# Spreading out the key work of later batches and reordering the head of a fused attention and MLP kernel

## The chip, the cores and the metric

The kernel runs on one core of one Trainium2 chip. The metric is the device time of one execution in microseconds (us), smaller is better. A time is the median of four to six timed executions (of one for m_csplit); a profile is what the hardware profiler recorded of one execution, and its span, from the first to the last instruction, is some 2 us shorter than the time. TensorE (PE in the profile) is the matrix engine, VectorE is DVE, ScalarE is ACT, GpSimd is POOL, and SP is the engine that issues most DMA transfers.

One thing has to be known about TensorE to follow this document. It has two clocks, and in every trace here the fast one was granted only some time after TensorE had begun to work. The trace holds a record of each grant. In the kernel before, pairs of 64-column passes start 107 ns apart up to 10.5 us and 57 ns apart from 10.6 us. I call the moment of the grant "the release" and the time before it "cold".

## The reference

Attention with a polynomial sketch, without softmax, then a two-layer MLP with the ELU activation. Four batches, four heads, 1088 rows, head dimension 32, sketch size r = 8.

```python
def phi(x):                                   # x: (b, h, s, 32)
    a = np.einsum('rd,bhsd->bhsr', S1, x)
    b = np.einsum('rd,bhsd->bhsr', S2, x)
    return np.einsum('bhsi,bhsj->bhsij', a, b).reshape(*x.shape[:-1], 64)
q_p, k_p = phi(q), phi(k)
kv  = np.einsum('bhsf,bhsd->bhfd', k_p, v)
z   = np.sum(k_p, axis=2)
num = np.einsum('bhsf,bhfd->bhsd', q_p, kv)
den = np.einsum('bhsf,bhf->bhs', q_p, z)[..., None] + 1e-06
x   = (num / den).transpose(0, 2, 1, 3).reshape(4352, 128)
h   = x @ w_in                                # 128 -> 2048
g   = np.where(h > 0, h, np.exp(np.minimum(h, 0)) - 1)
out = g @ w_out                               # 2048 -> 128
```

Nearly all the arithmetic is in the MLP. The attention decides when the MLP can start, and it must then be slipped in between the MLP's matmuls without making them wait.

## The kernel before

The kernel issues every instruction in a fixed order by hand. It has a head, which brings the first batch to its first MLP group, and a body of steps, each of two MLP matmul groups, one of each layer (1.72 us each), plus small pieces of attention work that are hung on numbered steps.

The head:

```python
def keep_warm(n, cols=256):                    # fillers: their results are never read
    for i in range(n):
        nc.tensor.matmul(idle[:, :cols], some[:, :P], some[:, :cols], skip_group_check=True)
...
eps = const.tile([1, 8, D + 1], F32, name="eps")      # one row: 1e-6 in the denominator's column
...
load_hd(nc.sync, "k", k, 0, 0, KT)             # keys of batch 0: two loads, runs of 1152 and 1024 B
load_hd(nc.scalar, "k", k, 0, KT, NT)
load_hd(nc.sync, "q", q, 0, 0, 8, slice(0, 1))
load_hd(nc.scalar, "q", q, 0, 0, 8, slice(1, 2))
load_v(0)
...
keep_warm(3)
keep_warm(1, 160)
sps = psum.tile([P, 512], F32, name="sps", tag="aux")
nc.tensor.matmul(sps[:, :2 * R], Sx[:]..., ident[:2 * R, :2 * R])
make_SX()                                      # one more matmul, 8 rows
...
def x0_eps():                                  # starts the sums of the first queries with 1e-6
    xps = []
    for tt in range(2):
        p = psum.tile([P, 512], F32, name="x0ps", tag="h", bufs=4)
        nc.tensor.matmul(p[:, :8 * (D + 1)], some[:1, :P], eps[:].rearrange("p m d -> p (m d)"),
                         start=True, stop=False, skip_group_check=True)
        xps.append(p)
    return xps
...
x0 = x0_eps()                                  # also serves as a filler
transp(kT, "k", 0, 0, KT)                      # VectorE: keys, two halves
transp(kT, "k", 0, KT, NT)
KF(0)                                          # TensorE: key features (abp in the profile)
KF_out(0)                                      # ScalarE: copies of them
transp(qT, "q", 0, 0, 8)                       # VectorE: first queries
KO(0, 0)                                       # VectorE: outer products (kp), group by group
q1_first()                                     # TensorE: query features (abqp)
KO(0, 1)
KO(0, 2)
RA(0)
RB(0)
q2_first()                                     # VectorE: outer product of the queries (qp)
for i in range(3):
    KA(0, i)                                   # TensorE: sums of keys times values (kv)
KC(0)
KZ1(0)
KS0()
q4_first()                                     # TensorE: transposes (qtp)
q5_first(x0)                                   # TensorE: x0ps, then x
mm1_first()                                    # first MLP matmul
```

The body. RA and RB are the first two steps of splitting a weight that arrives as 64-bit numbers; RC is the rest, and its flag sends its last step to GpSimd:

```python
for n, i in ((2, 3), (3, 4), (4, 6), (5, 5), (6, 7), (8, 8), (10, 9), (12, 10)):
    ...
    at(n, RC, i, i > 6)

for b, (n_t, n_f, n_o, n_a, n_z, n_q) in enumerate(
        ((3, 5, (6, 7), 8, 10, 9), (11, 12, (13, 14), 19, 20, 21), (17, 18, (20, 21), 22, 24, 25)), 1):
    at(n_t, transp, kT, "k", b, 0, NT)          # VectorE
    at(n_f, KF_late, b)                         # TensorE, 16 passes of 288 columns
    late(n_f, KF_late_out, b)                   # two VectorE transposes
    for half in range(2):
        at(n_o[half], KO_late, b, half)         # VectorE outer products
    at(n_a, KA_late, b)
    ...
```

## Time and profile before

| | kernel before |
|---|---|
| timed runs | 283.95 us (282.7 to 284.42) |
| span of the profile | 282.1 us |
| release of the TensorE clock | 10.59 us |
| first MLP matmul | 17.81 us |
| first 512-column MLP group | 19.62 us |

The prediction below shows the waits, the chain and the stretches of this profile. One more view is TensorE's own timeline. Its columns are start, duration, engine, source line, operation, output<-inputs, rows*columns of the weights, shape, and number of instructions; in brackets is the idle time ahead of it and who ended it.

```profile
5.59 1.96 PE L554 MATMUL x0ps<-eps,some 1*128 1x264 f32 x4
7.48 2.08 PE L298 MATMUL abp<-Sab,kT 128*64 128x64 f32 x33
...
10.34 2.66 PE L397 MATMUL kv<-v,kp 128*64 128x64 f32 x72
...
14.53 2.00 PE L569 MATMUL x0ps<-kvz,qpT 128*128 128x66 f32 x16
```

TensorE is never idle for long in this head. The 72 kv matmuls begin at 10.34, a quarter of a microsecond before the release, and so take 2.66 us.

### The profile page before, as it was taken

The numbers are of one execution on the slowest core, as the hardware profiler recorded it, in microseconds if no ns is written. First come the engines' busy times: TensorE is split into PE (matmuls) and PEld (weight loads), VectorE is DVE, ScalarE is ACT, GpSimd is POOL, SyncE is SP. The second block draws the span as 40 slices with busy tenths as digits, with TensorE's granted clock in tenths as the row PEclk, the third lists the DMA queues.
The fourth block names the chain that finished last, engine by engine and source line by source line (L and its number), as shares of the span: only waits on it lengthen the run. The fifth ranks groups of instructions, "written<-read, shape, count | busy, mean of one in ns | idle before, by whom it ended". The sixth has DMA issues, their size and how long they took to land.

```text
span 282.1 us, 3800 instructions
## 1 busy us (share of the span) xinstructions
PE 273.7 (97%) x1348; PEld 138.4 (49%) x1348; DVE 178.7 (63%) x319; ACT 179.8 (64%) x337; POOL 20.9 (7%) x55
## 2 busy tenths in 40 slices
PE   8999998999979999999999999999999999999994
PEld 6874333543443545444444444444444444444694
DVE  6788999998947695366635663456445734573442
ACT  2368966676546564666756665666566666667682
POOL 4070004333000000000000000000000000000000
PEclk9999999999999999999999999999999999999999
DMA  6994790010002200002000100020002000110020
GB/s 180 342 330 138 206 261 14 15 67 0 0 2 34 43 1 2 0 4 35 3 0 9 29 2 0 0 33 5 0 2 37 0 1 0 23 17 0 5 33 19
DMA packets 25474, 13.35 MB, mean 47 GB/s; under 512 B 18416, under 2 KB 23664, under 8 KB 25456
## 3 DMA queue, kind: packets, MB, share of 16 engines
q1 hardware_dynamic: 24944, 12.66, 17.5%
q10 hardware_dynamic: 512, 0.46, 0.5%
q8 instruction: 10, 0.16, 0.3%
q14 instruction: 8, 0.07, 0.1%
HBM read 10.88 MB, written 2.23 MB: 46 GB/s over the span
## 4 chain that ended last, share of the span: by engine, by line
PE 87%; DVE 8%; issue 1%; ACT 1%; POOL 1%; POOLq 0%; DVEq 0%
PE h L661 37%; PE o L698 36%; PE ol L721 3%; PE qps L627 2%; DVE gg L685 2%; PE kvl L340 1%; PE idle L221 1%; DVE kp L282 1%; PE qps L492 1%; POOL raw L122 1%; PE x0ps L569 1%; DVE raw L117 1%; PE h L668 1%; PE x0ps L554 1%; DVE W L112 1%
## 5 line engine op out<-in xcount | busy, mean ns | idle before, releaser
L685 DVE SCALAR_TENSOR_TENSOR gg<-e,h 128x512 f32<-128x512 f32 (+1 forms) x144 | 93.2, 656 | 89.5 <-ACT e L679 89.3
L661 PE MATMUL h<-xg,W 128*128 128x512 f32 (+1 forms) x284 | 127.0, 569 | 1.5 <-POOL W L123 1.1
L677 ACT ACTIVATE e<-h 128x512 f32<-128x512 f32 (+1 forms) x144 | 81.1, 564 | 72.6 <-PE h L661 72.4
L698 PE MATMUL o<-gg,W 128*128 128x512 f32 x256 | 121.7, 598 | 0.0
L679 ACT ACTIVATE e<-e 128x512 f32<-128x512 f32 (+1 forms) x144 | 87.3, 606 | 4.6
L661 PEld LDWEIGHTS h<-xg,W 128*128 128x128 f32 x284 | 53.4, 190 | 63.7 <-issue 51.8
L698 PEld LDWEIGHTS o<-gg,W 128*128 128x128 f32 x256 | 47.4, 190 | 56.3 <-issue 55.2
L104 ACT ACTIVATE W<-W,ebias 128x256 uint32<-128x256 uint32 (+1 forms) x11 | 6.6, 600 | 5.7 <-DVE W L99 5.6
L520 DVE TENSOR_TENSOR qp<-an,abw 128x1024 f32<-128x1024 f32 (+1 forms) x9 | 9.3, 1047 | 0.3
L627 PE MATMUL qps<-qpT,kvp 64*64 64x256 f32 (+3 forms) x136 | 7.4, 339 | 1.5 <-DVE qpT L617 1.5
L721 PEld LDWEIGHTS ol<-W,gg 128*128 128x128 f32 x64 | 8.1, 192 | 0.3
L617 DVE STREAM_TRANSPOSE qpT<-qp 128x1024 f32<-128x1024 f32 (+1 forms) x7 | 8.1, 1161 | 0.0
L721 PE MATMUL ol<-W,gg 128*128 128x128 f32 x64 | 8.1, 275 | 0.0
L282 DVE TENSOR_TENSOR kpl<-abk 128x1280 f32<-128x1280 f32 (+1 forms) x6 | 8.1, 1346 | 0.0
L627 PEld LDWEIGHTS qps<-qpT,kvp 64*64 64x64 f32 x136 | 4.7, 132 | 6.6 <-issue 3.1
L122 POOL TENSOR_TENSOR raw<-raw,tiny 128x512 f32<-128x512 f32 x4 | 5.4, 1338 | 32.3 <-DVE raw L117 32.3
L502 DVE STREAM_TRANSPOSE abw<-qps 128x256 f32<-128x256 f32 (+1 forms) x14 | 5.2, 407 | 2.0 <-ACT xg L639 2.0
L117 DVE SCALAR_TENSOR_TENSOR raw<-raw 128x256 f32<-128x256 uint32 (+1 forms) x11 | 6.0, 549 | 0.3
L112 DVE SCALAR_TENSOR_TENSOR W<-raw,W 128x256 uint32<-128x256 uint32 (+1 forms) x11 | 5.9, 541 | 0.0
L705 DVE STREAM_TRANSPOSE ob<-o 128x512 f32<-128x512 f32 x8 | 5.7, 710 | 0.1
L639 ACT COPY xg<-qps 128x256 f32<-128x256 f32 x12 | 3.9, 373 | 2.8 <-PE qps L492 2.8
L123 POOL TENSOR_TENSOR W<-raw,W 128x512 f32<-128x512 f32 x4 | 5.4, 1342 | 0.3
(118 smaller groups left out, 136.2 us busy)
## 6 DMA issues: line engine op xcount, KB each, us to landing
raw<-in_moe_w_in_dram SPq DMA_DIRECT2D x8, 256.0 KB, 5.8
raw<-in_moe_w_out_dram SPq DMA_DIRECT2D x8, 256.0 KB, 5.9
hd_k<-in_k_dram SPq DMA_DIRECT2D x3, 544.0 KB, 8.3
hd_q<-in_q_dram SPq DMA_DIRECT2D x3, 544.0 KB, 3.2
out_dram<-ob SPq DMA_DIRECT2D x40, 32.0 KB, 1.7
v<-in_v_dram SPq DMA_DIRECT2D x4, 288.0 KB, 9.0
v<-in_v_dram SPq DMA_DIRECT2D x4, 256.0 KB, 9.1
hd_k<-in_k_dram SPq DMA_DIRECT2D x1, 288.0 KB, 3.7
```

The lines of the kernel that those rows point to most:

```text
L112: nc.vector.scalar_tensor_tensor(d, hi, 0x80000000, d, op0=AND, op1=OR)
L117: nc.vector.scalar_tensor_tensor(lo.bitcast(F32), lo, 2.0 ** -32, raw[:, :, 1], op0=MUL, op1=ADD)
L122: nc.gpsimd.tensor_mul(mant, mant, _ap(tiny[:], [[0, dst.shape[1]]]))
L282: nc.vector.tensor_mul(dst, _ap(a_, list(a_.ap[1:]) + [[0, R]]), _ap(b_, [b_.ap[1], [0, R], b_.ap[2]]))
L520: nc.vector.tensor_mul(qp[g][:, h], _ap(a_, list(a_.ap[1:]) + [[0, R]]), _ap(b_, [b_.ap[1], [0, R], b_.ap[2]]))
L627: nc.tensor.matmul(ps[e][64 * g2:64 * g2 + 64, 64 * k:64 * (k + m)], kvp[r, b, f, g2].rearrange("p c d -> p (c d)"), qpT[g][r, n * g2 + 2 ...
L661: nc.tensor.matmul(hs[g, cp][c][:, :n], W[:, cp, c * P:c * P + P], xg[g][:, :n])
L677: nc.scalar.activation(e, hs[g, cp][c][:, :n], RELU, scale=-1.0)
L679: nc.scalar.activation(e, e, EXP, scale=-1.0)
L685: nc.vector.scalar_tensor_tensor(gs[g, cp][:, c, :n], es[g, cp][:, c, :n], -1.0, hs[g, cp][c][:, :n], op0=ADD, op1=MAX)
L698: nc.tensor.matmul(ops[g][:, :n], W[:, cp, (2 + c) * P:(3 + c) * P], gg[:, c, :n], start=(first and c == 0), stop=(last and c == 1))
L721: nc.tensor.matmul(ops[g][i][:], gg[:, c, i * P:i * P + P], W[:, cp, (2 + c) * P:(3 + c) * P], start=(first and c == 0), stop=(last and c ...
```

## The change

It has two intents. In the body, VectorE is full up to 80 us and has room afterwards, so the key work of batches 2 and 3 goes to later steps, batch 1 gets its features in a way that needs no VectorE transpose, some small GpSimd work moves, and the last rounding step goes from GpSimd to VectorE for most weights. In the head, the first group of keys is loaded, transposed and turned into features ahead of the rest, so that VectorE's chain of outer products can start 1.5 us earlier; the place of x0ps in front is given to a short filler, and x0ps follows the query features.

```diff
-    load_hd(nc.sync, "k", k, 0, 0, KT)
-    load_hd(nc.scalar, "k", k, 0, KT, NT)
+    load_k0(nc.sync, 0, 0, 4)                  # four loads, by tiles: runs of 512 and 640 B
+    load_k0(nc.scalar, 1, 0, 4)
+    load_k0(nc.sync, 0, 4, KT)
+    load_k0(nc.scalar, 1, 4, NT - KT)
...
-    keep_warm(1, 160)
+    keep_warm(1, 64)
...
     def KF(b):
-        ps = [psum.tile([P, 512], F32, name="abp", tag="aux") for _ in range(2)]
+        ps = [psum.tile([P, 512], F32, name="abp", tag="h", bufs=4) for _ in range(2)]
...
+    def KF_second(b):                          # batch 1: 36 passes of 64 columns, keys as weights
+        ...
+            nc.scalar.copy(ab[:, :, t]..., ps[j][:, :64 * n]...)
...
-    x0 = x0_eps()
-    transp(kT, "k", 0, 0, KT)
-    transp(kT, "k", 0, KT, NT)
+    keep_warm(1, 96)
+    transp(kT, "k", 0, 0, 8)
+    transp(kT, "k", 0, 8, NT)
     KF(0)
     KF_out(0)
+    KO(0, 0)
     transp(qT, "q", 0, 0, 8)
-    KO(0, 0)
     q1_first()
+    x0 = x0_eps()
     KO(0, 1)
+    q2_first()
     KO(0, 2)
     RA(0)
     RB(0)
-    q2_first()
-    for i in range(3):
-        KA(0, i)
+    KA(0, 0)
+    KA(0, 1)
+    q4_first(0)
+    KA(0, 2)
...
-        at(n, RC, i, i > 6)
+        at(n, RC, i, i == 7)
...
-            ((3, 5, (6, 7), 8, 10, 9), (11, 12, (13, 14), 19, 20, 21), (17, 18, (20, 21), 22, 24, 25)), 1):
+            ((3, 5, (7, 9), 10, 11), (15, 16, (17, 18), 19, 20), (18, 20, (24, 25), 27, 29)), 1):
...
-        at(n_f, KF_late, b)
-        late(n_f, KF_late_out, b)
+        if b == 1:
+            at(n_f, KF_second, b)
+        else:
+            at(n_f, KF_late, b)
+            late(n_f, KF_late_out, b)
```

Cut are the index function for the new key positions, the moves of make_SWp, KZ3, KS, make_SXh and of the query transposes, and a change of one accumulation bank.

More of the change, by code (lines that the diff above doesn't have):

```diff
@@ L79, in load_hd, with key_at, load_k0 @@
                       src[b].rearrange("h (a c t) d -> (h a) c t d", a=32, c=2)[:, c, t0:t1, :])
+    def key_at(u, i):
+        return 4 * u + i if i < 4 else 4 * (1 + u) + u + i
+    def load_k0(eng, u, i0, i1):
+        if ("k", 0) not in hd:
+            hd["k", 0] = work.tile([P, 2, NT, D], F32, name="hd_k", tag="hd_k")
+        p = key_at(u, i0)
+        eng.dma_start(hd["k", 0][:, :, p:p + i1 - i0, :],
+                      k[0].rearrange("h (a c t) d -> (h a) c t d", a=32, c=2)[:, :, u * KT + i0:u * KT + i1, :])
     def load_v(b, engs=(nc.sync, nc.sync)):
@@ L297, in KF @@
             for u in range(2 if i + KT < NT else 1):
-                nc.tensor.matmul(to[64 * u:64 * u + 64, :], kT[b][:, u * KT + i, :],
+                nc.tensor.matmul(to[64 * u:64 * u + 64, :], kT[b][:, key_at(u, i), :],
                                  Sab[:].rearrange("p h y -> p (h y)"),
@@ L301, in KF @@
         abps[b] = [where[i] for i in (0, 4, 8)]
+    def KF_second(b):
+        ps = [psum.tile([P, 512], F32, name="abp", tag="aux") for _ in range(2)]
+        for i in range(KT):
+            for u in range(2):
+                nc.tensor.matmul(ps[i // 5][64 * u:64 * u + 64, 64 * (i % 5):64 * (i % 5) + 64],
+                                 kT[b][:, u * KT + i, :], Sab[:].rearrange("p h y -> p (h y)"),
+                                 skip_group_check=True, tile_position=(0, 64 * u))
+        ab = feats[b] = work.tile([P, 2, KT, H, R], F32, name="abk", tag="abk", bufs=2)
+        for j in range(2):
+            t = slice(0, 5) if j == 0 else slice(5, KT)
+            n = t.stop - t.start
+            nc.scalar.copy(ab[:, :, t].rearrange("p x t h r -> p x (t h) r"),
+                           ps[j][:, :64 * n].rearrange("p (m x r) -> p x m r", x=2, r=R))
     def KF_late(b):
@@ L333, in KA_late @@
     def KA_late(b):
-        kv = kv_ps[b] = psum.tile([P, 512], F32, name="kvl", **(dict(tag="aux") if b == 1 else dict(tag="o1", bufs=1)))
+        kv = kv_ps[b] = psum.tile([P, 512], F32, name="kvl", **(dict(tag="aux") if b == 1 else dict(tag=f"o{3 - b}", bufs=1)))
         ab = feats.pop(b)
@@ L539, in q2_first, with q4_first @@
         outer(qp[0][:], abw[0][:])
-    def q4_first():
-        qpT[0] = work.tile([P, 4, 2, P], F32, name="qpT", tag="qpT", bufs=2)
-        for tt in range(2):
-            p = psum.tile([P, 512], F32, name="qtp", tag="aux")
-            for m in range(4):
-                r = 8 * tt + 2 * m
-                nc.tensor.transpose(p[:, m * P:m * P + P], qp[0][:, r:r + 2].rearrange("p t i j -> p (t i j)"), ident[:])
-            nc.scalar.copy(qpT[0][:, 2 * tt:2 * tt + 2].rearrange("p t g s -> p (t g s)"), p[:])
+    def q4_first(tt):
+        if tt == 0:
+            qpT[0] = work.tile([P, 4, 2, P], F32, name="qpT", tag="qpT", bufs=2)
+        p = psum.tile([P, 512], F32, name="qtp", tag="aux")
+        for m in range(4):
+            r = 8 * tt + 2 * m
+            nc.tensor.transpose(p[:, m * P:m * P + P], qp[0][:, r:r + 2].rearrange("p t i j -> p (t i j)"), ident[:])
+        nc.scalar.copy(qpT[0][:, 2 * tt:2 * tt + 2].rearrange("p t g s -> p (t g s)"), p[:])
     def x0_eps():
@@ L752 @@
     KS0()
-    q4_first()
+    q4_first(1)
     q5_first(x0)
@@ L768 @@
     q5_second()
-    make_SWp()
-    KZ3(0)
-    KS(0)
-    make_SXh()
     keep_warm(1)
@@ L799 @@
             late(n - 1, RB, i)
-        at(n, RC, i, i > 6)
-    for b, (n_t, n_f, n_o, n_a, n_z, n_q) in enumerate(
-            ((3, 5, (6, 7), 8, 10, 9), (11, 12, (13, 14), 19, 20, 21), (17, 18, (20, 21), 22, 24, 25)), 1):
-        at(n_t, transp, kT, "k", b, 0, NT)
-        at(n_f, KF_late, b)
-        late(n_f, KF_late_out, b)
+        at(n, RC, i, i == 7)
+    late(2, make_SWp)
+    late(3, KZ3, 0)
+    late(3, KS, 0)
+    late(4, make_SXh)
+    for b, (n_t, n_f, n_o, n_a, n_z) in enumerate(
+            ((3, 5, (7, 9), 10, 11), (15, 16, (17, 18), 19, 20), (18, 20, (24, 25), 27, 29)), 1):
+        at(n_t, transp, kT, "k", b, 0, NT)
+        if b == 1:
[3 more added lines that the diff above has]
+            late(n_f, KF_late_out, b)
         for half in range(2):
@@ L814 @@
         late(n_z, KZ3, b)
-        at(n_q, transp, qT, "q", b, 0, NT)
+    late(6, transp, qT, "q", 1, 0, NT)
+    at(21, transp, qT, "q", 2, 0, NT)
+    at(30, transp, qT, "q", 3, 0, NT)
     at(13, queries, None, 2)
```

## The prediction

> **What bounds the kernel now.** I read the page first, then the waits of the TensorE, the chain that ended last, and the busy time by stretches. The page says that TensorE is busy nearly all the time, but that figure is a mean over stages. The waits say where it really stood still:
>
> ```profile
> PE 273.7 (97%) x1348; PEld 138.4 (49%) x1348; DVE 178.7 (63%) x319; ACT 179.8 (64%) x337; POOL 20.9 (7%) x55
> ...
> PE qps L627 <- DVE qpT L617: 1.5, 1, 1.5
> PE idle L221 <- DVE warm L144: 1.2, 1, 1.2
> PE h L661 <- POOL W L123: 1.1, 1, 1.1
> PE h L661 <- DVE W L125: 0.3, 1, 0.3
> ```
>
> The columns are who waited, for whom, microseconds in total, times, longest. From 80 us on there is no wait at all: that part is a stream of big matmuls, 1.72 us per four passes, and only work taken off TensorE could shorten it. What scheduling can win lies ahead of 80 us. By the slots (a group of four should start 1.72 us after the last), the three late waits cost 0.54 us (the group due at 31.45 starts at 31.99), 1.31 us (due 46.67, starts 47.98) and 1.65 us (due 77.42, the small matmuls start at 79.07): 3.5 us in all. The stretches say who makes TensorE wait there:
>
> ```profile
> 40.00:48.00 8.00, 6.85 (x17) 2.68 (x15) 7.93 (x13) 5.54 (x10) 3.51 (x2) 1.00 0.34 67
> 70.00:80.00 10.00, 8.51 (x53) 4.04 (x54) 9.21 (x16) 6.14 (x11) 0.00 (x0) 1.00 0.00 0
> 80.00:100.00 20.00, 20.00 (x160) 9.20 (x152) 11.59 (x21) 10.78 (x21) 0.00 (x0) 1.00 0.17 28
> ```
>
> After the window the columns are its length, then busy us of PE, PEld, DVE, ACT, POOL. VectorE is full up to 80 us (7.93 of 8, 9.21 of 10) and has 8.4 of 20 us free right after. The POOL row shows why the second wait is so long: the last step of one weight's rounding runs there, and its first instruction takes twice its usual time beside a VectorE outer product:
>
> ```profile
> 44.34 2.22 POOL L122 TENSOR_TENSOR raw<-raw,tiny 128x512 f32<-128x512 f32 x1 [19.23 <-DVE raw L117]
> 46.64 1.29 POOL L123 TENSOR_TENSOR W<-raw,W 128x512 f32<-128x512 f32 x1
> 52.43 1.04 POOL L122 TENSOR_TENSOR raw<-raw,tiny 128x512 f32<-128x512 f32 x1 [4.50 <-DVE raw L117]
> ```
>
> The head (up to 17.8 us, the first MLP matmul) is a chain of short dependent steps:
>
> ```profile
> 5.79 1.76 PE x0ps L554 x4
> 7.55 1.07 PE abp L298 x16
> 8.65 0.38 ACT ab L373
> ...
> 9.06 2.69 DVE kp L282 x3
> 11.74 0.20 DVE W L99
> 11.95 1.14 DVE qp L282
> ```
>
> The key features (abp) wait for the filler x0ps, though both transposed key halves are ready at 6.73; then VectorE works without a gap from 9.06 to 15.0.
>
> **What the Trainium skill says.** "TensorE: Matmul & The Clock Gate", Part 1, says the array runs at half rate until a window of about 3.4 us has been busy, that the windows run freely, and that the moment of release varies from run to run. The trace agrees: filler passes of 256 columns start 427 ns apart, pairs of 64-column passes 107 ns apart until 10.5 us and 57 ns apart from 10.6 us. "TensorEngine Tiling (Array Packing)", Key Properties, says that tiles work independently: the two 64-row halves of the key features start 7 ns apart, so I count pairs. "SBUF — State Buffer", Who interferes with whom, says that a VectorE instruction with two SBUF inputs blocks a GpSimd instruction that reads SBUF: the 2.22 against 1.04 us above agrees. "DMA: Bandwidth & Descriptors", Specifications, puts the smallest full-rate run at 512 B; the new key loads have runs of exactly 512 and 640 B (4 or 5 tiles of 32 floats) in place of 1152 and 1024, so I do not expect a worse rate; no run here shows it yet.
>
> **The change, part by part.**
>
> *Head, filler and loads.* The last warm-up filler shrinks from 160 to 64 columns a pass; its two passes end at 4.12 instead of 4.44. The next matmul (4.58) needs Sx, ready at 4.36, so it can start near 4.42: 0.15 us won, and Sab comes at 5.08 instead of 5.22. The key loads become four. Before, the two landed at 4.88 and 5.58 us. The first halves are 128 KB each and should land by about 4.8, the second by about 5.6 (an estimate from the 60 packets per 0.2 us and queue that the trace shows at full flow). So the first transpose starts at 5.22, limited by Sab, takes 0.67, and the features of group 0 can start at 5.95 instead of 7.49. Eight pairs of 107 ns, a copy and its latency took 1.57 us before (7.49 to 9.06); the first outer product then starts at 7.52, 1.54 us earlier.
>
> *Head, what is given back.* Now VectorE runs the first outer product (1.14), the query transpose (0.59) and the second outer product (1.14): 7.52, 8.66, 9.25, free at 10.39. But the query features wait for the transpose until 9.38; TensorE executes in order and stands still from 7.9 to 9.38. Their 16 cold passes and the copy took 1.7 us before (9.26 to 10.95), so they are ready at 11.07: VectorE waits 0.7 us, and qp is finished at 12.3 instead of 13.08. And x0ps (four passes: 1.76 us cold, 0.9 warm) now lies between the query features and the key-value sums, which take 36 pairs: 2.1 us warm, 3.9 cold. Three cases. Clock released before 9.4 us: the sums end near 13.4, and the first x0 matmul starts about 14.05 against 14.53, so −0.5. Clock released at 10.6 as before: x0ps ends 11.5, the sums (with four transposes between) 14.3, their copies 14.9, so the x0 matmul comes 0.4 later. Clock released near 14: x0ps ends 12.2, the first 16 pairs 14.0, the rest of the sums 15.7, copies 16.4: +1.9. The hole from 7.9 to 9.38 lies in just the window (7.17 to 10.58, if windows are 3.41 long and end at the release) that released the clock before; this makes the late case likely. I choose chances of 0.35, 0.35 and 0.3: −0.18 + 0.14 + 0.57 = **+0.5 us**.
>
> *Moved GpSimd work.* SWp, KZ3, KS and SXh go into later steps. GpSimd's own order hardly changes by it, for nothing else stands between; these start by their inputs, as before at 15.2 us. Only one VectorE reduction of 0.17 us leaves the crowded place at 24.35. About **−0.1**, off the first wait.
>
> *Batch 1.* Its key features are made with the keys as weights: 36 passes, 18 pairs of 57 ns, about 1.1 us warm against 0.65 for the 16 passes of 288 columns: **+0.5 us on TensorE**, on the path. In exchange two VectorE transposes (0.85 us with latency, 0.76 of its time) become two ScalarE copies of about 0.4 us; ScalarE is busy 5.54 of 8 us there. The outer products leave steps 6 and 7 for 7 and 9, so the one of 1.4 us no longer stands beside the GpSimd step: its 2.22 falls to about 1.04. With 0.8 us less VectorE work ahead, the weight of 47.93 should be ready near 45.9; TensorE wants it at 46.67 or later. The wait of 1.31 us vanishes: **−1.3**.
>
> *Rounding.* Three of four last rounding steps move from GpSimd to VectorE, 0.6 us issue to issue each: +1.8 us of VectorE work between 48 and 68 us.
>
> *Batches 2 and 3.* Transpose 1.25, two feature transposes 0.76, outer products 1.4 + 1.14: 4.5 us of VectorE work for batch 2 leave steps 11 to 14 for 15 to 18; batch 3 goes from 17–22 to 18–25. VectorE's steps 8 to 14 then sum to 3.5 + 2.7 + 3.5 + 2.0 + 3.5 + 4.4 + 2.4 = 22 us (activations 1.2 a step, a rounding 2.3, a query chain 3.1) beside TensorE's 26. So qpT comes about 2.5 us earlier and the third wait, 1.65 us, vanishes: **−1.65**. Steps 15 to 22 sum to about 24 us of VectorE beside 33 of TensorE, so no new wait there.
>
> *Sum.* 0.5 − 0.1 + 0.5 − 1.3 − 1.65 = −2.05: 283.95 becomes **281.9 us**.
>
> **Rivals.** (1) *The clock takes the head's gain.* If the release comes only in a window ending at 17 us, everything small in the head runs at half rate, and the head costs 3 us or more: 284 to 285. For it: the new hole and the one-row x0ps, which may not count as activity. Against it: the releasing window is free-running, so the mean cannot be far in one direction. (2) *VectorE stays the bound to step 8.* The row of 40 to 48 us has it 99% busy; if the copies on ScalarE or the query transpose brought forward to step 6 delay the rounding, the second wait keeps half its size: 282.6. (3) *The work moved to steps 15 to 22 makes new waits,* above all at step 18, with transpose, outer product and activations (3.6 us against a slot of 3.43): a loss of 0.5 to 1 us; the slack of two steps between activation and second matmul speaks against it. (4) *The head gains in full,* because the clock is released early: 1.5 us better than my sum for the head, 280.4.
>
> **Range and chances.** The body gives −2.0 to −3.2, the head −0.7 to +3, and the timed runs of before spread over 1.7 us. I take 279.2 to 284.4. Faster by over 2% means 278.3 or less, 5.7 us: all three waits (3.5) and over 2 us of the head together; 0.05. Slower by over 2% would need 289.6, for which I see no mechanism: 0.015.
>
> **What would show it.** Right: no TensorE wait on POOL W or on qpT; the first outer product near 7.5 us; 18 pairs for batch 1's features of 1.1 us; VectorE less full from 48 to 80 us, fuller from 80 to 110. The chain of the head should show x0ps after the query features, and the start of the first MLP matmul, 17.8 before, says at once which clock case it was. Wrong: a first MLP matmul before 16.8 or after 20 us; a remaining wait on the rounding of the fourth or fifth weight; any wait after 80 us; key loads landing after 6 us.

## The result and the profile after

| | before | after |
|---|---|---|
| timed runs | 283.95 us (282.7 to 284.42) | 287.29 us (286.44 to 287.45) |
| span of the profile | 282.1 us | 285.4 us |
| clock records | released 10.59 | released 4.51, taken back 7.92, released 18.16 |
| first MLP matmul | 17.81 us | 22.93 us |

The ratio after over before is 1.0118 (95% interval 1.0081 to 1.0156). A ratio here is the mean time of one kernel's fast runs over the mean of the other's fast runs of the same rounds, so it is not quite the ratio of the medians in the table. As a measured difference it is 1.2% slower, outside the range that I had given.

The first lines of the profile of after, and its row of the granted clock in 40 slices of 7.1 us:

```profile
PE 276.7 (97%) x1370; PEld 140.8 (49%) x1370; DVE 178.7 (63%) x320; ACT 180.7 (63%) x339; POOL 12.1 (4%) x49
...
PEclk9579999999999999999999999999999999999999
```

TensorE is busy for 97% again, and the busy time has even grown by 3.0 us, from 273.7. Batch 1's 20 further passes are about half a microsecond of it; the rest is the same work running longer. The clock row shows where: slices 2 and 3 have 5 and 7 tenths. The time before the first record counts as full in this row, so a kernel that is cold up to its first release, like before, shows nines there; the records have to be read too.

The waits of TensorE, after:

```profile
PE abp L312 <- DVE kT L249: 2.2, 2, 2.0
...
PE abqp L559 <- DVE qT L249: 0.5, 1, 0.5
PE qps L656 <- DVE qpT L646: 0.4, 1, 0.4
```

The wait for POOL W (1.1) is gone and the wait for qpT has fallen from 1.5 to 0.4: the body does what it should. In exchange there are two new waits in the head, for keys and for queries. The stretches of the body, after (window, its length, then busy us of PE, PEld, DVE, ACT, POOL, granted clock, DMA share, GB/s):

```profile
40.00:48.00 8.00, 8.00 (x53) 3.94 (x52) 7.68 (x17) 5.72 (x12) 0.51 (x1) 1.00 0.99 243
...
70.00:80.00 10.00, 10.00 (x34) 4.23 (x33) 8.07 (x15) 6.21 (x11) 0.00 (x0) 1.00 0.00 0
80.00:100.00 20.00, 19.64 (x175) 9.18 (x174) 15.15 (x22) 12.73 (x24) 0.00 (x0) 1.00 0.17 28
```

TensorE is busy for all of 40 to 48 and 70 to 80 us, against 6.85 of 8 and 8.51 of 10. VectorE has fallen from 9.21 to 8.07 in the one and risen from 11.59 to 15.15 between 80 and 100 us, where it has room. From the first 512-column group to the output group after the second queries of the body (19.62 to 80.60 before, 24.75 to 82.94 after) TensorE needs 58.19 us against 60.98: the body has won 2.8 us there. So the loss is all in the head. TensorE's timeline of the head, after:

```profile
5.74 0.69 PE L312 MATMUL abp<-Sab,kT 128*64 128x64 f32 x16 [0.23 <-DVE kT L249]
8.40 1.33 PE L312 MATMUL abp<-Sab,kT 128*64 128x64 f32 x18 [1.97 <-DVE kT L249]
10.22 1.12 PE L559 MATMUL abqp<-Sab,qT 128*64 128x64 f32 x16 [0.49 <-DVE qT L249]
11.28 2.12 PE L583 MATMUL x0ps<-eps,some 1*128 1x264 f32 x4
13.33 3.68 PE L426 MATMUL kv<-v,kp 128*64 128x64 f32 x64
...
19.67 1.53 PE L598 MATMUL x0ps<-kvz,qpT 128*128 128x66 f32 x12
```

Group 0's features do start at 5.74, as intended. Then TensorE stands still for 2 us until the second half of the keys is there. After that everything is cold: x0ps takes 2.1 us and now stands on the path, and the 64 kv matmuls take 3.68 us. The first MLP matmul comes 5.1 us later than before, made up of 3.0 us up to the first kv matmul (10.34 to 13.33), 2.15 from there to the second x0ps (4.19 to 6.34), and nothing after it.

The chain of after names what the hole waited for (start, duration, what):

```profile
2.04 5.51 DMA hd_k<-in_k_dram
...
8.27 1.18 DVE kp L296
```

The last key load takes 5.51 us from issue to landing. In before, both loads landed by 5.6 us. VectorE runs in order, so the first outer product, whose input was ready near 7, waits behind the transpose of the late keys and starts at 8.27.

### The profile page after: what moved, and what is told of

The parts are those of the page before. It is cut to its first block, busy times and chain, and to the rows that moved or that the text cites. A ratio compares the mean times of both kernels' runs of the same rounds, so it can differ in the third digit from the quotient of the medians.

```text
span 285.4 us, 3835 instructions
## 1 busy us (share of the span) xinstructions
PE 276.7 (97%) x1370; PEld 140.8 (49%) x1370; DVE 178.7 (63%) x320; ACT 180.7 (63%) x339; POOL 12.1 (4%) x49
## 4 chain that ended last, share of the span: by engine, by line
PE 86%; DVE 5%; ACT 3%; DMA 2%; issue 1%; ACTq 0%; POOL 0%
PE h L690 37%; PE o L727 37%; PE ol L750 3%; PE qps L656 2%; DMA hd_k<-in_k_dram 2%; PE kvl L369 1%; DVE gg L714 1%; ACT e L708 1%; PE kv L426 1%; ACT e L706 1%; PE qps L521 1%; PE x0ps L583 1%; DVE W L137 1%; PE xps L634 0%; DVE raw L129 0%
## 5 line engine op out<-in xcount | busy, mean ns | idle before, releaser
L249 DVE STREAM_TRANSPOSE kT<-hd_k 128x1088 f32<-128x1088 f32 (+2 forms) x5 | 5.4, 1079 | 1.9 <-DMA hd_k<-in_k_dram 1.9
L137 DVE SCALAR_TENSOR_TENSOR W<-raw,W 128x256 f32<-128x256 f32 (+1 forms) x10 | 5.4, 537 | 0.3
L235 PE MATMUL idle<-some 128*128 128x256 f32 (+2 forms) x12 | 4.4, 516 | 1.2 <-DVE warm L158 1.2
L249 DVE STREAM_TRANSPOSE qT<-hd_q 128x1088 f32<-128x1088 f32 (+2 forms) x5 | 5.4, 1081 | 0.0
```

The costliest lines, as they stand in the source:

```text
L137: nc.vector.scalar_tensor_tensor(dst, mant, 2.0 ** -20, dst, op0=MUL, op1=MUL)
L249: nc.vector.transpose(dst[b][:, t0:t1, :].rearrange("p t (a c) -> p c t a", c=2), hd[x, b][:, :, t0:t1, :])
```

## The experiments

All kernels named here gave correct results. The kernel before had medians of 283.1, 283.87 and 283.05 us in the later sessions, so I compare ratios.

### Which half of the change costs

**a_body** keeps the old head and takes the new body; **b_head** does the reverse.

```diff
 # a_body against after: the head of the kernel before
-    load_k0(...)  x4                       +    load_hd(...)  x2
-    keep_warm(1, 64) ... keep_warm(1, 96)  +    keep_warm(1, 160) ... x0 = x0_eps()
-    KO(0, 0) ahead of transp(qT, ...)      +    the order of before, to mm1_first()
 # b_head against before: the same lines the other way round
```

> The head of before with the body of after (MLP steps, batches 1 to 3, moved GpSimd work). Theory H (all of the loss is in the head, the body gains): the profile of after reaches the ninth group's matmuls with 2.8 us less waiting and work between the second MLP group and 83 us, of which 0.65 us of work is only moved later, so 281.9 us, about 2 under before; no TensorE wait on POOL W, and one of under 0.5 us on qpT. Rival B (the body loses too, by the extra 36 passes and the rounding on VectorE): 284 us or more.

> The head of after (key loads, features, order, fillers) with the body of before. Theory H: before plus 5 us, the difference of the first MLP matmuls in the two profiles (22.93 against 17.81): 288 to 289.5 us. Rival B: 286 or less, for then the head would be only a part of the loss. If both parts add, a_body and b_head together differ from twice before by the 3.3 us of after.

Measured: a_body 282.08 us, ratio 0.9946 (0.9903 to 0.9989). b_head 288.56 us, ratio 1.0188 (1.0164 to 1.0212), release at 17.13. The new head costs 1.9% and the new body wins 0.5%. By these ratios the two parts together come to 3.8 us over twice before, against 3.3 us for after, so they add within half a microsecond. Later, on another chip, the same a_body kernel was run once more as **a_body_2**:

> The kernel a_body again, on this chip, as the base of the three others: 282.1 us; runs with a clock released before 8 us near 281, the others near 282.8.

Measured: 283.03 us, ratio 0.9984 (0.9943 to 1.0025). So the body's gain in the total is between nothing and 1%, and its repeat alone would not have shown it; the profile of the stretch above does, because it looks where the gain is made. In the profiles, a_body's stretch from the first 512-column group to 80 us is 58.16 us, 2.8 less than before; 1.0 us comes back later (0.65 of it the feature matmuls of batch 2, which now lie there), and 0.5 is a release at 12.42 in place of 10.59. That leaves 1.3 us, which is also what the spans say (282.1 and 280.8).

### In the head: the late keys or the clock

Two theories were open. By the first, the holes that the late keys make are the cost. By the second, what matters is what TensorE does in the time that decides on the clock: the one-row x0ps does not count as work for the release, and the new order puts it and the holes where the release would have come. **c_twoloads** undoes only the loads; **d_x0front** undoes only the place of x0ps.

```diff
 # c_twoloads against after
-    load_k0(...) x4
+    load_hd(nc.sync, "k", k, 0, 0, KT)
+    load_hd(nc.scalar, "k", k, 0, KT, NT)
 # d_x0front against after
-    keep_warm(1, 96)
+    x0 = x0_eps()
...
     q1_first()
-    x0 = x0_eps()
```

> After with the keys in two loads and their old positions; the rest of the new head stays. Theory L (the late second key half, landed at 7.55 us against 5.58, makes the loss): both halves are transposed by 6.7, and the time falls by 1.5 to 2 us to 285.5. Theory O (the order on TensorE makes it: x0ps ahead of the key-value sums, at half clock): the first outer product comes at 8.3 us as in after, the query features at 10.2 as in after, and the time stays within 0.7 us of after.

> After with x0ps put back in front of the key features in place of the small filler; four loads and the rest of the new head stay. Theory O: x0ps fills a stretch in which TensorE waits for keys anyway; the sums start near 11.4 us instead of 13.3, and the time falls by 2 us or more, to 285 or less. Theory L: no change, 287 us.

Measured: c_twoloads 287.23 us, ratio 1.0146 (1.012 to 1.0172); d_x0front 283.97 us, ratio 1.0026 (0.998 to 1.0072). With the old loads nothing is won. Their keys are in time (no hole at 6.4; the first outer product begins at 7.68 and the query features at 9.68, half a microsecond earlier than I expected), but VectorE then runs the first outer product ahead of the query transpose, as the new order says, and the hole only moves. The timeline of c_twoloads:

```profile
6.56 1.15 PE L310 MATMUL abp<-Sab,kT 128*64 128x64 f32 x32 [0.26 <-DVE kT L247]
9.68 1.12 PE L557 MATMUL abqp<-Sab,qT 128*64 128x64 f32 x16 [1.96 <-DVE qT L247]
...
12.78 3.68 PE L424 MATMUL kv<-v,kp 128*64 128x64 f32 x64
```

The clock was released at 5.0, taken back at 8.41, and released again at 18.65, so kv is cold once more.

In d_x0front, moving four instructions forward, in the place of two filler passes, wins 3.3 us against c_twoloads of the same session (2.6 to 3.3 against after, by the ratios or by the medians): x0ps is off the path, and the lasting release comes at 11.51 (after one at 4.68 that was taken back at 8.10). This profile is of the fastest of the four runs, 282.76.

```profile
9.72 1.13 PE L559 MATMUL abqp<-Sab,qT 128*64 128x64 f32 x16 [0.63 <-DVE qT L249]
10.59 2.47 PE L426 MATMUL kv<-v,kp 128*64 128x64 f32 x64
```

The same 64 kv matmuls take 2.47 us in place of 3.68. The four runs of d_x0front go from 282.76 to 285.22. The two fast ones have the same mean granted clock, 0.994, the slow ones 0.985 and 1.000, so it is likely that the moments of release, which vary from run to run, still decide over 2 us.

### What the clock counts

In every profile the records of the clock start at distances that are multiples of 3.413 us, so the decision is made once in such a window. In after they give this (window, length, PE busy, granted clock, DMA share, GB/s):

```profile
4.51:7.92 3.41, 1.69 (x22) 1.00 1.06 242
7.92:11.33 3.41, 2.44 (x35) 0.50 1.07 283
11.33:14.75 3.42, 3.42 (x31) 0.50 1.08 363
14.75:18.16 3.41, 3.41 (x51) 0.50 1.08 368
```

After the first window, half empty, the clock is taken back. The third, 11.33 to 14.75, has TensorE busy throughout (3.42 of 3.42), and yet no release follows it. Up to 13.3 its work is the one-row x0ps. The fourth, all kv and transposes over 64 or 128 rows, is followed by the release at 18.16. The busy share of the profile alone is thus not what the clock looks at.

To test it, **e_rows** gives x0ps 128 rows, of which 127 are zero, so that the result stays the same at the same number of columns. **e_fill** also puts three fillers into the hole.

```diff
 # e_rows against after
-    eps = const.tile([1, 8, D + 1], F32, name="eps")
+    eps = const.tile([P, 8, D + 1], F32, name="eps")
-    nc.gpsimd.memset(eps[:, :, D:], 1e-6)
+    nc.gpsimd.memset(eps[:1, :, D:], 1e-6)
-            nc.tensor.matmul(p[...], some[:1, :P], eps[:]...)
+            nc.tensor.matmul(p[...], some[:, :P], eps[:]...)
 # e_fill: that, and in KF
+            if i == 3:
+                keep_warm(3)
```

> After with x0ps formed over 128 rows (127 of them zeros) in place of one row: same passes, same columns, same place. In the profile of after the clock was released at 4.5 us, taken back at 7.9 and given again only at 18.2, though TensorE ran x0ps and sums without a gap from 11.3 to 14.7. Theory R (a matmul with one row hardly counts as activity): the next release comes one window of 3.4 us earlier, near 14.7, the sums run at full rate, and the time falls by about 1 us to 286.3. Rival (rows do not matter, only time): 287.3, and the release as late as before.

> After with the 128-row x0ps and three filler matmuls in the hole that waits for the second key half. Theory K (the clock is the larger part of the head's loss): the clock stays released from about 4.5 us or comes back by 11, the sums take 2.1 us instead of 3.7 and x0ps 0.9 instead of 2.0, and the time falls by 2.5 to 3 us to 284.5. Rival P (the place of x0ps costs whatever the clock does): half of that or less, 286 or more.

Measured: e_rows 286.18 us, ratio 1.0093 (1.006 to 1.0125); e_fill 284.33 us, ratio 1.0037 (1.001 to 1.0063), release at 10.56 and first MLP matmul at 20.16. e_fill is faster than after by 2.3 us by the ratios (3.0 by the medians), although its three fillers hold the second part of the key features back to 10.21 us, from 8.40: an earlier release is worth more than that. e_rows is no clean proof. Its interval overlaps that of after, and its profile has the windows elsewhere (release at 16.63), with the holes in two of them.

The cleaner pair is on the old head, where there is no hole. **r_rows** is a_body with the 128-row x0ps. It can be set beside **g_pool**, which has the same head with the one-row x0ps and whose windows happened to lie 0.29 us apart; what g_pool changes in the body follows below.

> The kernel a_body with x0ps formed over 128 rows instead of one; in the old head it stands from 5.6 to 7.4 us. Theory R (one-row matmuls do not count for the clock): with them counted TensorE is busy enough in every window that starts after 5.3 us, so the release lies between 8.7 and 12.1 us instead of 10.5 to 13.9, and the mean time falls by 0.5 to 1 us to 281.3. Rival (rows do not matter): 282.1 and releases as in a_body.

Measured: 281.18 us, ratio 0.9932 (0.989 to 0.9975), against 0.9984 for a_body_2 in the same session; their intervals overlap, so the profiles have to say more. The windows of g_pool and then of r_rows:

```profile
4.64:8.06 3.42, 3.23 (x51) 1.00 1.08 270
8.06:11.47 3.41, 2.92 (x58) 0.50 1.06 336
```

```profile
4.93:8.34 3.41, 3.41 (x58) 1.00 1.09 273
8.34:11.75 3.41, 2.84 (x80) 1.00 1.07 356
```

Both were released early (4.64 and 4.93), before their x0ps ran, so its rows had no part in that; I had expected the release of r_rows between 8.7 and 12.1. The windows that follow are nearly full and full by the profile (3.23 and 3.41 us busy), but in g_pool about 1 us of it is one-row x0ps, and the clock is taken back at 8.06; in r_rows it stays until about 1 us before the end. This is one profile each, so chance could still have a part.

A count over all seventeen profiles takes, for each window, the time in which TensorE ran matmuls with 64 rows or more in their weights, each counted until the next one starts. On the slow clock, all 21 windows that ended in a release had such work for 0.81 or more of their length. The windows without a release had it for 0.79 or less, with two exceptions, and in both the 128-row x0ps ran for over half of the window: 0.86 in e_rows and 0.84 in w_newhead (a kernel described below). Here are these two, with a less busy window of d_x0front between them that was followed by a release (window, length, PE busy, granted clock, DMA share, GB/s; before the first record of a trace the clock column shows 1.00, so e_rows and w_newhead are cold here):

```profile
9.80:13.22 3.42, 2.93 (x22) 1.00 1.07 344
```

```profile
8.10:11.51 3.41, 2.78 (x52) 0.50 1.07 308
```

```profile
3.62:7.03 3.41, 3.41 (x12) 1.00 0.96 239
```

So it is shown that windows full of work were refused when a good part of it had one row (1.00 busy in after, and also in before and a_body with the old head). It is not shown that 128 rows make x0ps count in full: on the slow clock they did not bring the release. Rows may not be what matters: x0ps streams zeros in all but 8 of its 264 columns, where the fillers are all ones, and no run varied the values. The border near 0.8 is a count of these runs, with ends of matmuls that are modelled.

**s_eps8** tried the opposite: f_late (below) with x0ps shrunk to the eight columns that matter, and a filler over 128 rows in the time so won.

```diff
-            nc.tensor.matmul(p[:, :8 * (D + 1)], some[:1, :P], eps[:]...)
+            nc.tensor.matmul(_ap(p[:, D:], [[D + 1, 8]]), some[:1, :P], eps[:],
...
     x0 = x0_eps()
+    keep_warm(1)
```

> A version that should beat both: old head, new body, batch 1's features as before (f_late), and x0ps writes only the 8 columns that need a value, 4 short passes in place of 1.76 us, with one 128-row filler matmul after it that ends when the second key half is transposed (6.75). The key features should start at 6.8 instead of 7.49 and the clock be released a window earlier in most runs: 280.9 us, against 281.9 of f_late. If the key features are not what the head waits for, no change: 281.9.

Measured: 282.30 us, ratio 0.9951 (0.9912 to 0.999), the ratio of f_late, so a miss. I had counted the four passes by their eight columns. They still take 0.86 us in all: each comes with a load of 128 columns of weights, and those four loads start 0.21 us apart in the trace. So the filler began at 6.38 and ended late, and the key features began at 7.53, no earlier than with the long x0ps.

### Why the second key half was late

The prediction took runs of 512 and 640 B for as good as 1024 and 1152. Two explanations were open: the number of loads (four issues in place of two), or the length of the runs. **m_csplit** is a_body with four loads that are cut the other way, so that the runs keep their length.

```diff
 # m_csplit against a_body
-    load_hd(nc.sync, "k", k, 0, 0, KT)
-    load_hd(nc.scalar, "k", k, 0, KT, NT)
+    load_hd(nc.sync, "k", k, 0, 0, KT, slice(0, 1))
+    load_hd(nc.scalar, "k", k, 0, KT, NT, slice(0, 1))
+    load_hd(nc.sync, "k", k, 0, 0, KT, slice(1, 2))
+    load_hd(nc.scalar, "k", k, 0, KT, NT, slice(1, 2))
```

> The kernel a_body with its key loads also cut in four, but by the other dimension: runs stay 1152 and 1024 bytes, 128 packets a load, so the number of packets is as in two loads. Theory S (the 512-byte runs, twice as many packets, make the keys late): all keys land by 5.6 to 5.9 us as in a_body. Theory N (the number of loads in the queues makes it): the last lands after 6.5 us.

Measured (one look): 282.29 us, and the four loads landed at 3.59, 3.94, 4.58 and 4.78, against 3.90, 4.28, 6.22 and 7.55 in after. So it is the runs and not the number of loads. The other profiles agree: the last key load landed between 7.04 and 7.96 in all six kernels with the short runs, and by 5.6 in all eleven with the long ones. The ACT queue's transfers from 0 to 10 us carry the same bytes in every kernel (packets, MB, share of 16 engines); first after, then m_csplit:

```profile
q10 hardware_dynamic: 704, 0.40, 16.9%
```

```profile
q10 hardware_dynamic: 448, 0.40, 12.7%
```

Before has 432 packets and 11.4%. The same 0.40 MB take a third to a half more of the engines' time when cut in short runs. Two more numbers belong to it. The issue instructions take longer with more runs: 0.60 to 0.78 us each in after (256 runs each), 0.37 to 0.44 in m_csplit (128 runs each), so the last key load is issued about half a microsecond later. And the sixteen completions of after's last key load are spread from 4.98 to 7.55 us, where m_csplit's lie between 4.34 and 4.78: a few engines finish late, while value and query packets of other loads stand in the same queues. That the queues behind cause the spread is likely, but not shown.

### Parts of the body

**h_unspread** is a_body with batches 2 and 3 at their old steps. **g_pool** is a_body with the old GpSimd rounding. **f_late** is a_body with batch 1's features made in the old way.

```diff
 # h_unspread against a_body (with it, the accumulation bank of before)
-  ((3, 5, (7, 9), 10, 11), (15, 16, (17, 18), 19, 20), (18, 20, (24, 25), 27, 29)), 1):
+  ((3, 5, (7, 9), 10, 11), (11, 12, (13, 14), 19, 20), (17, 18, (20, 21), 22, 24)), 1):
 # g_pool against a_body
-        at(n, RC, i, i == 7)
+        at(n, RC, i, i > 6)
 # f_late against a_body
-        if b == 1:
-            at(n_f, KF_second, b)
-        else:
-            at(n_f, KF_late, b)
-            late(n_f, KF_late_out, b)
+        at(n_f, KF_late, b)
+        late(n_f, KF_late_out, b)
```

> The kernel a_body with batches 2 and 3 back at the steps of before (keys at 11 to 14, and 17 to 21). Prediction's sum: the wait on qpT of 1.3 us more comes back (0.4 is left in a_body, 1.5 was in before), with VectorE nearly full from 60 to 80 us: 283.2 to 283.5. Rival (the spreading won nothing): 282.1.

> The kernel a_body with the last rounding step of weights five to eight back on GpSimd (three more instructions pairs there, 1.8 us less on VectorE between 48 and 68 us). Theory V (what made the POOL wait was the outer product beside it, which has moved): no TensorE wait on POOL W, and 282.1 us as a_body, within 0.5. Rival G (the long GpSimd chain itself is too slow): a wait on POOL W of 1 us or more comes back, 283 or more.

> The kernel a_body (old head, new body) with the key features of batch 1 made as before: 16 passes and two VectorE transposes in place of 36 passes and two ScalarE copies. My prediction's sum: 0.5 us less on TensorE's path, 281.6 against 282.1, if VectorE can take 0.76 us more at step 5. Rival (VectorE is the bound up to step 8): a wait for weights comes back and it is 282.5 or more.

Measured: h_unspread 284.18 us, ratio 1.0021 (0.9988 to 1.0054). The wait is back, whole; the waits of h_unspread and, below, of a_body:

```profile
PE qps L654 <- DVE qpT L644: 1.5, 1, 1.5
```

```profile
PE qps L654 <- DVE qpT L644: 0.4, 1, 0.4
```

So the spreading of batches 2 and 3 is what removes that wait. Of its loss in the profile's head, 0.6 us comes from a later release (13.62 against 12.42; first MLP matmul 18.88 against 18.28); in the timed runs the interval doesn't separate it from a_body.

g_pool 282.15 us, ratio 0.995 (0.9907 to 0.9994), the same as a_body, and no wait for POOL W in its profile. So the wait that stood there before was ended by moving the outer product away from beside the GpSimd step, and the move of the rounding to VectorE added nothing. The weight that TensorE waited for keeps its last step on GpSimd in every kernel here, also in after (the case i == 7). f_late shows the same with batch 1's features made in the old way: measured from the first MLP matmul, the GpSimd step began 0.16 us later than in before, took 1.05 us in place of 2.22, and the weight was ready 1.0 us earlier.

f_late 281.87 us, ratio 0.9951 (0.9912 to 0.999). I expected 0.5 us less than a_body by the matmuls saved; its interval contains that and contains nothing at all. It is not resolved.

### A version that beats both

**v_best** puts together the old head, the new body, the old features for batch 1, the 128-row x0ps, and moves make_SX (an 8-row matmul) from the cold start to after the query features. **w_newhead** tries the same repairs on the new head: after, with x0ps in front and over 128 rows and the late make_SX.

```diff
 # v_best against a_body; w_newhead has the same edits to eps, some and make_SX,
 # on the head of after with  keep_warm(1, 96) -> x0 = x0_eps()
-    make_SX()                       # after sps
...
     q1_first()
+    make_SX()
```

> Old head, new body, batch 1's features as before, x0ps over 128 rows, and the SX product (8 rows, not needed before 14 us) moved behind the query features, so that from 1.2 us on nearly all TensorE work is on full rows. If full-row activity is what releases the clock, every run is released by 8.1 us and stays so, the first MLP matmul comes near 16.8 us in all of them, and the median is 280.9 us with a spread under 1 us (a_body: 280.9 to 283.3). Rival (the release is luck of the window whatever the rows): median 282, spread 2 us.

> The same two repairs (128-row x0ps, late SX product) on the head of after with x0ps in front: what remains of the loss when order and clock are repaired is the late second key half. Theory D (the late keys still cost something): 1 to 1.5 us more than v_best, 282.2, with a hole before the second part of the key features. Rival (then the new head is as good as the old): 281.

Measured: v_best 280.87 us (six runs, 280.5 to 281.11), ratio 0.990 (0.9867 to 0.9934). All six runs lie at the level of a_body's fastest (280.91), within 0.6 us, where those of a_body spread over 2.0. (The spread alone says little: a_body_2's runs lie within 0.4 us, but at 283.0.) In its profile the clock was released at 5.08 and never taken back:

```profile
5.11 1.16 PE L580 MATMUL x0ps<-eps,some 128*128 128x264 f32 x4
...
6.78 1.15 PE L309 MATMUL abp<-Sab,kT 128*64 128x64 f32 x32 [0.25 <-DVE kT L247]
...
9.18 2.66 PE L423 MATMUL kv<-v,kp 128*64 128x64 f32 x72
```

The kv sums start at 9.18 in place of 10.34 and the first MLP matmul at 16.60 in place of 17.81. It is 1% faster than before by its ratio and 2.2% faster than after by the medians. This is what I expected, 280.9 us. But the window that ended in the release, from 1.67 to 5.08, has no x0ps in it, and no run separates the rows of x0ps from the later make_SX, so which of the two made the runs alike stays open.

w_newhead 286.32 us, ratio 1.0081 (1.0039 to 1.0123): a miss. The clock was released at 17.28 only. In its timeline TensorE runs on to 8.1 and then waits 0.27 us for the keys and 0.75 us for the queries before 10.43. These holes explain one refused window, 7.03 to 10.45. The windows before and after it were busy throughout and were refused too: 3.62 to 7.03, with the 128-row x0ps (shown above), and 10.45 to 13.86, with make_SX's 8-row matmuls in it (0.79 by the count). I had hoped that this run would give the cost of the late keys at full clock. It does not: late keys cost through the clock too, and what they would cost alone stays open.

## Why the prediction was wrong

**The step that failed** is the head's term, "I choose chances of 0.35, 0.35 and 0.3: −0.18 + 0.14 + 0.57 = **+0.5 us**". Measured, the first MLP matmul came 5.1 us later in the profiles (at 22.93; "after 20 us" was among the signs of being wrong), and b_head was 1.9% slower, some 5.3 us. With +5.1 in place of +0.5 the sum of my other terms gives 286.5, close to the 287.29 measured. Within that term three things went wrong.

- *The keys.* "The first halves ... should land by about 4.8, the second by about 5.6", and for the short runs "I do not expect a worse rate". The first halves came at 3.90 and 4.28, earlier than I said; the second at 6.22 and 7.55. m_csplit shows that the short runs did it. The rate behind the estimate, 60 packets per 0.2 us and queue, was also too high: in the trace of before one queue reaches 67 to 70 while it has most of the flow, but both together never more than 87. I had named "key loads landing after 6 us" among the signs of being wrong, and it was one. Of the 3.0 us up to kv, 0.9 is late features (abp goes on at 8.40 where it began at 7.49 before).
- *The place of x0ps.* I had it in the sum as 0.9 to 1.76 us between the query features and kv, and it took 2.05 us of the path. I saw that it was a filler, but I priced its move by its length only. Its old place cost nothing on the path, as the keys weren't there yet.
- *The clock.* I gave the release near 14 us a chance of 0.3 and a cost of 1.9 us, and put a release at 17 us among the rivals. It was at 18.16 in after, 17.13 in b_head and 18.65 in c_twoloads. Rival 1 named just these things, "the new hole and the one-row x0ps, which may not count as activity", and I talked it down with "the releasing window is free-running, so the mean cannot be far in one direction". That argument needs windows that can release wherever they lie. Here each window of the profile from 4.51 to 14.75 has a hole or one-row work in it, and the four timed runs of after lie within 1.0 us although their mean clocks (0.980, 0.997, 1.000 and 0.981) say that their windows lay differently. The rival's own price, 284 to 285, was still too small, because it took the late clock alone and left x0ps and the keys at my figures.

**What was right** is the body, though there too with sizes off. The wait for POOL W vanished (−1.3 predicted; the stretch from 40 to 48 us has TensorE busy throughout). The wait for qpT went from 1.5 to 0.4 and not to nothing, so its term was −1.1 and not −1.65. Batch 1's features took 1.2 us for 18 pairs, as said. By profile the stretch up to 80 us won 2.8 us, and 1.0 came back later, where the feature matmuls of batch 2 now lie; my sum for the body had taken no account of matmuls that leave one stretch and arrive in another. "Right" also was VectorE's easing before 80 us and its filling after it. The rivals about VectorE (2 and 3) did not come about: no new wait from step 15 on appears in the waits of after (what is left of the wait for qpT now falls at 81 us). The −0.1 for the moved GpSimd work did not come: the first of the three waits is as long in after as in before (0.31 us in the waits, 0.47 by the slots; the prediction's slot of 31.45 should have been 31.52, one group of 1.72 us after 29.80).

**The rounding was moved for nothing.** The cause that I gave for the second wait, the outer product beside the GpSimd step, held: that step takes 1.04 us in after. The move of the other rounding steps to VectorE, which I counted as work of 1.8 us there, wins nothing: g_pool keeps them on GpSimd and has no such wait either.

**The gain that the head was to bring** did not come with prompt keys either. In after the queries' outer product (qp) began at 11.79, against 11.87 in before: what the earlier first outer product won (8.27 against 9.06), the wait for the query features (0.39 us) and the late transposes gave back. In c_twoloads, with keys in time, qp began at 11.24 and so ended near 12.4, about as predicted (12.3). But the sums, behind x0ps and cold, began at 12.78 against 10.34, and the time was no better.

## What to carry to other kernels

A filler is not only there to fill: before moving one, ask what the clock will see in its old place and in its new one, for an engine that was busy throughout with one-row work was not granted the fast clock here. More rows are worth a try and no sure cure: with 128 rows r_rows kept a fast clock that it already had, while e_rows and w_newhead were still refused it. Cut a load in the direction that keeps its contiguous runs long, above all where the second piece is what the next engine waits for. When a change has two halves, time each alone: here a gain of half a per cent was hidden under a loss of almost two.

## What the Trainium skill lacked or had wrong

- "TensorE: Matmul & The Clock Gate", Part 1, says that the clock is released after a busy window of about 3.4 us and that the windows run freely; the runs agree (distances in multiples of 3.413 us). It doesn't say what counts as busy. Here 11.33 to 14.75 us was filled without a gap, to 13.3 us by a one-row matmul, and was refused; with 128 rows r_rows kept its early release (4.93 us) where g_pool, with one row, lost it at 8.06, but with 128 rows, mostly of zeros, e_rows was refused after 9.80 to 13.22 too.
- The same section puts the loss of the warm-up below 1% of a typical kernel's span and advises against fitting to it. Here the place of four passes decided 3.3 us between two kernels of one session, 287.23 and 283.97 (1.2%), by the path and the clock together, a pair that does not separate the share of the clock.
- "DMA: Bandwidth & Descriptors", Specifications, has full rate from 512 B on. The same 0.40 MB of the ACT queue took 16.9% of the engines' time with 512 B key runs and 11.4 to 12.7% with 1024 B, and the last key load landed at 7.55 us in place of 4.78.
- "DMA: Bandwidth & Descriptors" calls the generation of descriptors small in its account of the gpsimd path. The loads here were issued by SP and ACT, for which it gives no such figure: a load with 256 runs held the issuing engine for 0.60 to 0.78 us, one with 128 runs for 0.37 to 0.44.
